# A retention layer with a gated feed-forward layer: two running sums moved ahead, two groups opened together, seven half-size products reordered

## The chip, the cores and the metric

The kernel runs on one core of a Trainium2 chip. The metric is the device time of one execution in microseconds (us). A core has engines that run side by side, each with a queue that it works off in order: TensorE (PE in the profile; its weight loads are PEld), VectorE (DVE), ScalarE (ACT), GpSimd (POOL) and SyncE (SP), which issues most transfers. They wait for each other through semaphores. TensorE writes into PSUM, which has eight banks; VectorE and ScalarE carry results out of it.

## The reference, cut to what matters

```python
scores = scale * np.matmul(q, k.transpose(0, 1, 3, 2))       # q, k, v: 8 x 8 x 576 x 64
Dmat = np.where(rel >= 0, gamma ** rel, 0.0)                 # rel = row - column, gamma per head
attn_out = np.matmul(scores * Dmat, v)
x = attn_out.transpose(0, 2, 1, 3).reshape(4608, 512)
out = (x @ w_a) * (x @ w_b) @ w_out                          # 512 -> 1536 -> 512
```

## The kernel before, in words

**Retention by groups.** The 4608 rows are cut into 18 groups of 256. Fourteen and two more are halves of a batch's first 512 rows; groups 15 and 17 (`LEFT`) collect the last 64 rows of four batches each. In a group, the rows of one 64-row part meet each other through masked scores, and meet all earlier rows through a state, a running sum of key times value products. So a group needs these sets of small TensorE products, each 64x64 on a quarter of the array:

- `keyed` (line 646): the key-value products `kv`, into two PSUM banks of the pool `ps_ffn`. VectorE then adds them up in four steps, `add(0)` to `add(3)` (line 690, tile `sums`). The two banks come free when the last two steps have read them. ScalarE turns sums into `states`.
- `matched` (line 725): the scores `sc`, which VectorE masks (line 743, tile `sT`).
- `open_outputs` (line 796): the products of queries and states open the output `o`; behind it ScalarE reads two columns (`fence`, line 803), for which the next set waits.
- `close_outputs` (line 806): the products of masked scores and values finish `o`; ScalarE copies it to `xT` (line 819) later, when the code pops a list `later`.

`stretch(into, outof)` (line 828) issues such sets in one go: it opens the outputs of group `outof`, forms `kv` and `sc` of group `into`, and closes `outof`. A group in `LEFT` has no `kv`, so its stretch has only `sc` and the closing; `outof` is opened by a separate call, `open_alone`, some products earlier. Group 17 is opened and closed by two more calls.

**Feed-forward by blocks.** Blocks of 512 rows (and two of 256) follow each other on TensorE. For each of twelve columns F there are four products `pa` (line 1365) and four `pb` (line 1383), each 128x512; ScalarE copies `pa` to `ha` (line 1376) and VectorE multiplies `ha` with `pb` to `hT` (line 1388). `pa`, `pb`, `kv` and others share the four banks of `ps_ffn`. From row 1536 on, the second layer goes by seven half-size products (`rows_mixed`, tile `m`), fed by sums of `hT` on VectorE (`row_sums`, line 957, bf16, both operands in SBUF), and its results are put together on GpSimd (line 1046) and VectorE (lines 1056 and 1063). In the last two blocks (rows 3584 and 4096) pairs of columns of the first layer go by seven half-size products as well (`layer_mixed`): ways 1 to 7, into banks `lm` (ways 1, 6, 7, 4), `ls` (5, 3) and `la` (2). ScalarE keeps a copy after ways 1 (`straight`), 6 (`crossed`) and 5 (`less`), line 1205, and the next way into that bank waits for it. They use sums of weights (`combos`, line 1151) and of rows (`rows`, line 1168), made on VectorE.

**What sets the order.** The order on each engine is that of the code. A list `todo` names a place, counted in 128x512 products, for each stretch; the stretches are put between two columns F. VectorE's smaller work stands in `jobs`, each with a class and a cost, and `work(budget)`, called behind each `hT`, issues jobs of the lowest class until the budget of 1.0 is used. The four `add` steps cost 0.5 each and have the lowest class, so behind a stretch two of them go after the next `hT` and two after the one that follows. `ORDER_MIDDLE` and `ORDER` (lines 1236 and 1288) are the hand-written orders of the half-size products of the last two blocks.

Of the kernel before, what the change touches and what calls it, by code (L numbers as in the profile page):

```python
# [10 lines left out]
FP32 = mybir.dt.float32  # L11
# [7 lines left out]
def kernel(  # L19
# [10 lines left out]
    nc = tc.nc  # L30
# [7 lines left out]
    HP = H // 2  # L38
# [6 lines left out]
    NP = NTOK // 256  # L45
    LEFT = {NP - 3: 0, NP - 1: 1}
# [57 lines left out]
    ps_ffn = pool("ps_ffn", 4, PS)  # L104
    opening, ps_sc, ps_o = ExitStack(), {}, {}
# [39 lines left out]
    def half(i):  # L145
        return slice(64 * i, 64 * i + 64)
# [120 lines left out]
    def pair_tables(step):  # L267
# [6 lines left out]
        else:  # L274
            for h in (2 * step - 2, 2 * step - 1):
# [8 lines left out]
                for n in range(FIRST)]  # L284
    second = sum_pool.tile([128, FIRST, HP, 64], FP32, tag="sums",
                           name="second")
# [20 lines left out]
    later = []  # L307
# [5 lines left out]
    jobs, copies_due = [], []  # L313
# [18 lines left out]
    def settle():  # L332

        while later:
            later.pop(0)()
        for job in [job for job in jobs if job[0] in (0, 2)]:
            jobs.remove(job)
            job[2]()
        pass_on(math.inf)

    def flush():
        while later:
            later.pop(0)()
        work(math.inf)
        pass_on(math.inf)
# [379 lines left out]
    def matched(n):  # L725
        qkT = of(transposed, n)
        sc = [ps_sc[0].tile([128, HP, 2, 64], FP32, tag="sc", name=f"sc{on}")
              for on in (0, 1)]
        begun = Begun()
        for c in range(HP):  # L730
            for kp in (0, 1):
                for a, r in QUADS:
                    on = r ^ a
                    nc.tensor.matmul(sc[on][half(a), c, kp, :],  # L734
                                     qkT[half(on), 1, kp, c, half(a)],
                                     qkT[half(on), 0, kp, c, half(a)],
                                     start=begun.first(on, a), stop=True,
                                     skip_group_check=True)
        sT = st_pool.tile([128, 2, HP, 2, 64], BF16, tag="sT", name="sT2")
        scored[FIRST + n, "pair"] = sT  # L740

        def masked(on):
            nc.vector.tensor_tensor(  # L743
                sT[:, on].rearrange("p c k s -> p (c k) s"),
                sc[on].rearrange("p c k s -> p (c k) s"),
                mask3.unsqueeze(1).to_broadcast([128, 2 * HP, 64]),
                op=ALU.mult)
        return masked

    def from_states(n, o, begun):  # L750
        qkT = of(transposed, n)
        st = states_of.pop(n)
        first = first_of.pop(n, st[:, 0])
        for c in range(HP):
            for kp in (0, 1):
                for a, r in QUADS:
                    i = 2 * kp + a
                    if block_of(n, i) == 0:
                        continue
                    on = r ^ a  # L760
                    own = st[:, i] if i else first
                    nc.tensor.matmul(o[a][half(r), c, kp, :],  # L762
                                     own[half(on), c, :],
                                     qkT[half(on), 0, kp, c, half(a)],
                                     start=begun.first(a, r), stop=True,
                                     skip_group_check=True)

    def keys_into(n, o, begun):
        vb = of(natural, n)[1]
        sT = of(scored, n)  # L770
        for c in range(HP):
            for kp in (0, 1):
                for a, r in QUADS:
                    v0 = kp * DM + c * 128 + 64 * r
                    nc.tensor.matmul(o[half(r), a, c, kp, :],  # L775
                                     vb[half(a), v0:v0 + 64],
                                     sT[half(a), r ^ a, c, kp, :],
                                     start=begun.first(a, r), stop=True,
                                     skip_group_check=True)

    def rows_at(n, kp):

        x = x_of(place(n) * 256, 256)
        if n < MIXED:
            return x.rearrange("p c (q a s) -> p q a c s",
                               q=2, a=2)[:, kp]
        return x.rearrange("p c (k q a s) -> p q a c k s",
                           k=2, q=2, a=2)[:, kp]
# [4 lines left out]

    opened = {}

    def open_outputs(n):

        o = ps_o[0].tile([128, 2, HP, 2, 64], FP32, tag="o", name="o2")
        begun = Begun()
        from_states(n, [o[:, a] for a in (0, 1)], begun)  # L800

        kp = int(0 in (block_of(n, 0), block_of(n, 1)))
        nc.scalar.copy(fence, o[:, :, 0, kp, 0])
        opened[n] = o, begun

    def close_outputs(n):

        o, begun = opened.pop(n)
        keys_into(n, o, begun)

        def kept(kp):
            x = rows_at(n, kp)
            at = o[:, :, :, kp]
            if n < MIXED:
                by = qs_1[:, :, 128 * kp:128 * kp + 128].rearrange(
                    "p c (a s) -> p a c s", a=2)
                nc.vector.tensor_tensor(x, at, by, op=ALU.mult)
                return
            nc.scalar.copy(x, at.rearrange("p a c (s k) -> p a c k s", k=2))  # L819

        later.append(lambda: kept(0))
        later.append(lambda: kept(1))

    def open_alone(n):
        (settle if n >= NP - 2 else flush)()
        open_outputs(n)

    def stretch(into, outof):

        (settle if into == NP - 1 else flush)()  # L830
        if into == FIRST:
            ps_next("pair", 2)
        if into in LEFT:
            masked = matched(into)
            close_outputs(outof)
            later.append(lambda: masked(0))
            later.append(lambda: masked(1))
            return
        if into == 5:
            convert, convert_swapped = keyed(into, False,  # L840
                                             lambda: open_outputs(outof))
            pop()
            pop()
        else:
            if outof is not None:
                open_outputs(outof)
            convert, convert_swapped = keyed(into, outof is None)
        masked = matched(into)
        if outof is not None:
            close_outputs(outof)  # L850
        if into == 4:
            later.append(later.pop(1))
            behind.extend([lambda: masked(0), convert, lambda: masked(1)])
            behind.extend(convert_swapped(apart=True))
            return
        if into > MIXED:
            jobs.extend((0, 0.5, add) for add in later[:4])
            jobs.append((0, 0, lambda: copies_due.extend(
                [convert, convert_swapped])))
            jobs.extend((0 if into % 2 else 2, 0.7,  # L860
                         lambda on=on: masked(on)) for on in (0, 1))
            copies_due.extend(later[4:])
            later.clear()
            return
        later.append(lambda: (convert(), masked(0)))
        later.append(lambda: (convert_swapped(), masked(1)))
# [21 lines left out]
    begun = {}  # L888
# [281 lines left out]
    def layer_mixed(tok0, xT, hT):  # L1170
# [63 lines left out]

    MIDDLE = (NTOK - 1024,)
    ORDER_MIDDLE = (
        (1, 0), (5, 0), (2, 0), (6, 0), (1, 1), (3, 0), (7, 0), (5, 1),
        (2, 1), (6, 1), (4, 0), ("a", 4), (3, 1), (7, 1), ("b", 4),
        ("a", 5), (4, 1), ("b", 5)) + tuple(
            (w, F) for F in range(6, 12) for w in "ab")  # L1240
    SHARE_MIDDLE = {1: 0, 5: 0, 2: 0, 6: 0.4, 3: 0, 7: 0.4, 4: 0, "b": 1}
# [1 line left out]
    def middle_layer(tok0, xT, hT, sums):  # L1243
# [3 lines left out]
        for way, at in ORDER_MIDDLE:  # L1247
# [33 lines left out]
            if done == 5:  # L1281
# [3 lines left out]
            work(SHARE_MIDDLE[way])  # L1285
            yield last, way in ("b", 4) and not underway

    ORDER = ((1, 0), (5, 0), (2, 0), (6, 0), (1, 1), (3, 0), (7, 0), (5, 1),
             (2, 1), (6, 1), (4, 0), ("a", 4), (3, 1), (7, 1), ("b", 4),
             ("a", 5), (4, 1), ("b", 5),  # L1290
             (1, 3), (5, 3), (2, 3), (6, 3), (1, 4), (3, 3), (7, 3), (5, 4),
             (2, 4), (6, 4), (4, 3), ("a", 10), (3, 4), (7, 4), ("b", 10),
# [135 lines left out]
    fence = const.tile([128, 2], FP32)  # L1428
# [95 lines left out]
    starts, at = {}, 0.0  # L1524
# [60 lines left out]
    for n in range(8, NP, 2):  # L1585
        todo += [(starts[n] - (92 if n == 16 else 116 if n > 8 else 112), stretch, (n + 1, n)),
                 (starts[n] - (52 if n > 8 else 48), stretch, (n + 2, n + 1))
                 if n + 2 < NP else
                 (starts[n] - 52, close_outputs, (n + 1,))]
    todo += [(starts[n - 1] - 124, open_alone, (n - 1,)) for n in LEFT]  # L1590
    todo += [(starts[NP - 2] - 60, open_alone, (NP - 1,))]
    placed = {args[0]: at for at, fn, args in todo if fn is stretch}
    casts = {3: 116, 4: 116.15, 5: 141, 6: 200, 7: 253, 8: 283, 9: 376,
             10: 412}
# [12 lines left out]
             (411.95, store_held, (2,)), (412.3, load_pair, (11, (K, V))),  # L1607
             (458, load_pair, (12,)), (447, store_held, (2,)),
             (456, store_held, (2,))]
    LATE = 8, 8, 8, 50, 8  # L1610
    CAST_A, TURN_A, CAST_B, TURN_B = 96, 58, 96, 58
    for n in range(11, NP):
# [51 lines left out]
```

## Time and profile before

| what | value |
|---|---|
| time, median of 3 | 318.93 us (318.79 to 319.56) |
| time of the profiled execution | 318.84 us |
| span of its instructions | 317.1 us, 1.74 us less than its time |
| TensorE clock granted | 1.00 |
| blocks from row 1536, 2048, 2560, 3072, 3584, 4096 begin at about | 121, 154, 188, 220, 253, 284 us |
| `hT` products on VectorE (line 1388) | 96, mean 618 ns |
| `sums` (line 690) | 44, mean 423 ns |
| values by decay on GpSimd (line 615) | 17, mean 1729 ns |

The page counts busy time by engine and gives, for each group of instructions, the idle time before it and what ended it. The timeline lists an engine's instructions in order of time with their starts, and behind some of them in brackets how long the engine had been idle and for what; `issue` means that the profile shows no wait. The TensorE rows there merge instructions of one kind that follow each other (x4), so the distance of two starts tells how long the first kind held the array.

### The profile page before, as it was taken

To read this page: it belongs to the slowest core of one execution; us is meant where nothing else is said; L and a number is where in the kernel's file an instruction comes from. 1 tells how busy PE (TensorE), PEld (TensorE's weight loads), DVE (VectorE), ACT (ScalarE), POOL (GpSimd) and SP (SyncE) were. 2 spreads that over 40 slices of the span, in tenths; PEclk is the share of its full clock that TensorE was granted. 3 is DMA by queue.
4 is the path that set the end of the run, shared out by engine and by line. 5 is a ranking of instruction groups with operands and counts; after the bars stand their busy time and mean duration, and the time that the engine had idled before them with its cause. 6 is when DMAs were issued, how large, how long until landed. Compare 5 with 4: busy or idle time off the path is not lost.

```text
span 317.1 us, 9394 instructions
## 1 busy us (share of the span) xinstructions
PE 310.5 (98%) x3871; PEld 190.9 (60%) x3871; DVE 217.9 (69%) x426; ACT 150.5 (47%) x333; POOL 169.3 (53%) x187
## 2 busy tenths in 40 slices
PE   8999999999999999999999999999999999999995
PEld 3554457768544554548644775468446874587774
DVE  5845346767858572479668867787677886758873
ACT  6745346536435364454455535535434554335630
POOL 3990068654995678473796079605980350035313
PEclk9999999999999999999999999999999999999999
DMA  8999999999999999999999996983530030004004
GB/s 215 255 203 207 253 237 181 189 211 172 212 176 225 225 227 200 234 212 268 192 262 220 175 234 133 194 181 105 148 68 3 2 132 2 2 0 134 1 3 132
DMA packets 144795, 50.94 MB, mean 161 GB/s; under 512 B 126576, under 2 KB 141680, under 8 KB 144752
## 3 DMA queue, kind: packets, MB, share of 16 engines
q1 hardware_dynamic: 138272, 45.10, 71.2%
q0 software_dynamic: 5808, 4.72, 9.5%
q8 instruction: 30, 0.49, 0.7%
q10 hardware_dynamic: 672, 0.52, 0.5%
q14 instruction: 13, 0.11, 0.1%
HBM read 37.75 MB, written 9.44 MB: 149 GB/s over the span
## 4 chain that ended last, share of the span: by engine, by line
PE 90%; DVE 3%; DMA 2%; POOL 1%; SPq 1%; ACT 1%; issue 1%; DVEq 0%; ACTq 0%; POOLq 0%
PE pb L1383 23%; PE pa L1365 22%; PE m L1023 16%; PE po L1409 8%; PE lm L1198 3%; PE pa L1253 2%; PE pb L1253 2%; DMA vf<-in_v_dram 2%; PE o L762 2%; PE sc L734 2%; PE po L909 2%; PE ls L1198 1%; PE o L775 1%; PE kv L663 1%; SPq L182 1%; PE pb L1307 1%
## 5 line engine op out<-in xcount | busy, mean ns | idle before, releaser
L1388 DVE TENSOR_TENSOR hT<-ha,pb 128x512 bf16<-128x512 bf16 (+1 forms) x96 | 59.3, 618 | 55.6 <-PE pb L1383 46.8
L1383 PE MATMUL pb<-xT,wb_sb 128*128 128x512 bf16 (+1 forms) x384 | 87.0, 352 | 0.1
L1365 PE MATMUL pa<-xT,wa_sb 128*128 128x512 bf16 (+1 forms) x376 | 85.2, 352 | 0.0
L1376 ACT CAST ha<-pa 128x512 bf16<-128x512 f32 (+1 forms) x96 | 50.9, 531 | 68.3 <-PE pa L1365 65.7
L1383 PEld LDWEIGHTS <-wb_sb 128*128 128x128 bf16 x384 | 37.4, 98 | 36.2 <-issue 1.9
L1365 PEld LDWEIGHTS <-wa_sb 128*128 128x128 bf16 x376 | 35.7, 98 | 32.4 <-DVE sums L690 0.2
L1046 POOL TENSOR_TENSOR osb<-crossed,straight 128x512 f32<-128x512 f32 x12 | 15.2, 1269 | 73.5 <-ACT crossed L1035 73.3
L615 POOL TENSOR_TENSOR vb<-vf,vs 128x1024 bf16<-128x1024 f32 (+1 forms) x17 | 29.4, 1729 | 4.9 <-DMA vf<-in_v_dram 3.3
L578 POOL TENSOR_TENSOR qkb<-qf,qs 64x1024 bf16<-64x1024 f32 x12 | 23.3, 1942 | 15.8 <-DMA qf<-in_q_dram 11.1
L1023 PEld LDWEIGHTS <-hT 128*128 128x128 bf16 x288 | 28.1, 98 | 4.4
L1409 PE MATMUL po<-wo_sb,hT 128*128 128x512 bf16 x120 | 27.8, 379 | 0.0
L1023 PE MATMUL m<-wo_sums,hsum 128*128 128x256 bf16 x216 | 25.7, 273 | 0.0
L583 POOL TENSOR_TENSOR qkb<-qf,qs 64x512 bf16<-64x512 f32 x24 | 24.8, 1055 | 0.7
L957 DVE TENSOR_TENSOR hsum<-hT 128x512 bf16<-128x512 bf16 (+2 forms) x51 | 23.5, 489 | 0.3
L1023 PEld LDWEIGHTS <-hsum 128*128 128x128 bf16 x216 | 21.1, 98 | 2.5
L743 DVE TENSOR_TENSOR sT<-sc,mask 128x512 bf16<-128x512 f32 x30 | 19.8, 682 | 0.0
L690 DVE TENSOR_TENSOR sums<-kv,sums 128x256 f32<-128x256 f32 x44 | 18.6, 423 | 1.4
L608 POOL CAST qkb<-kf 64x512 bf16<-64x512 f32 (+1 forms) x34 | 19.1, 588 | 0.9
L604 POOL CAST qkb<-kf 64x1024 bf16<-64x1024 f32 (+1 forms) x17 | 16.2, 950 | 5.5 <-DMA kf<-in_k_dram 4.6
L819 ACT CAST xT<-o 128x512 bf16<-128x512 f32 x24 | 13.9, 588 | 10.3 <-PE o L775 10.3
L1409 PEld LDWEIGHTS <-hT 128*128 128x128 bf16 x120 | 11.2, 98 | 12.4
L1023 PE MATMUL m<-wo_sums,hT 128*128 128x256 bf16 x144 | 16.9, 273 | 0.0
(155 smaller groups left out, 434.7 us busy)
## 6 DMA issues: line engine op xcount, KB each, us to landing
qf<-in_q_dram SPq DMA_DIRECT2D x32, 256.0 KB, 4.5
vf<-in_v_dram SPq DMA_DIRECT2D x32, 256.0 KB, 5.2
kf<-in_k_dram SPq DMA_DIRECT2D x31, 256.0 KB, 4.8
out_dram<-osb SPq DMA_DIRECT2D x9, 512.0 KB, 3.4
out_dram<-osb SPq DMA_DIRECT2D x22, 128.0 KB, 2.9
wo_sb<-in_moe_w_out_dram POOLq DMA_DIRECT2D x3, 512.0 KB, 15.7
out_dram<-osb SPq DMA_DIRECT2D x6, 256.0 KB, 4.3
qf<-in_q_dram SPq DMA_DIRECT2D x8, 128.0 KB, 4.1
```

The costliest lines, as they stand in the source:

```text
L578: nc.gpsimd.tensor_tensor(per_head(qkb[0:64, Q]), per_head(t[0:64]), by[0:64].unsqueeze(2).to_broadcast([64, 2 * H, D]), op=ALU.mult)
L583: nc.gpsimd.tensor_tensor(per_head(qkb[64:128, Q])[:, 1 - r::2], per_head(t[64:128])[:, r::2], by[64:128, r::2].unsqueeze(2).to_broadcast( ...
L608: nc.gpsimd.tensor_copy(to[:, :, 1 - r], fro[:, :, r])
L615: nc.gpsimd.tensor_tensor(vb[:, e].rearrange("p (h d) -> p h d", d=D), t[:, e].rearrange("p (h d) -> p h d", d=D), decay[:, at], op=ALU.mult)
L743: nc.vector.tensor_tensor(sT[:, on].rearrange("p c k s -> p (c k) s"), sc[on].rearrange("p c k s -> p (c k) s"), mask3.unsqueeze(1).to_bro ...
L957: lambda e=ways[i]: nc.vector.tensor_tensor(*e[:3], op=e[3]))
L1023: nc.tensor.matmul(to, rows, cols, start=(begins and p == 0), stop=True, skip_group_check=True)
L1365: nc.tensor.matmul(pa[:, 0:n], wa_sb[:, c, fs], xT[:, c], start=(c == 0), stop=(c == NC - 1))
L1376: nc.scalar.copy(ha[:, 0:n], pa[:, 0:n])
L1383: nc.tensor.matmul(pb[:, 0:n], wb_sb[:, c, fs], xT[:, c], start=(c == 0), stop=(c == NC - 1))
L1388: nc.vector.tensor_tensor(hT[:, F, 0:n], has[F][:, 0:n], pb[:, 0:n], op=ALU.mult)
L1409: nc.tensor.matmul(po, hT[:, F, u * 128:(u + 1) * 128], wo_sb[:, F], start=(F == 0), stop=(F == NF - 1))
```

## The change

1. `NOW = 2`: in the stretches into groups after 6, the first two `add` steps are issued at the end of the stretch itself, ahead of the next `hT`, and the other two stay jobs.
2. In the stretches into groups 15 and 17 the outputs of both groups are opened: `outof` in two banks of `ps_ffn` (tiles `os0`, `os1`, with a `fence` and two copies each in place of one), `into` in the bank pair of `o`. Then come `sc` of `into` and the closing of `outof`. The calls of `open_alone` for groups 14, 16 and 17 go; group 17 is closed eight products earlier (`close_alone`).
3. In the first six pair-steps of `ORDER_MIDDLE` and of the first half of `ORDER`, way 2 of the first pair and ways 1 and 6 of the second come ahead of ways 5 and 3 of the first.

```diff
+    def open_outputs(n, apart=False):
+
+        if apart:
+            o = [ps_ffn.tile([128, HP, 2, 64], FP32, tag="ab", name=f"os{a}")
+                 for a in (0, 1)]
+        else:
+            o = ps_o[0].tile([128, 2, HP, 2, 64], FP32, tag="o", name="o2")
...
+        if apart:
+            for a in (0, 1):
+                nc.scalar.copy(fence[:, a:a + 1], o[a][:, 0, kp, 0:1])
+        else:
+            nc.scalar.copy(fence, o[:, :, 0, kp, 0])
...
+            if apart:
+                for a in (0, 1):
+                    nc.scalar.copy(x[:, a], o[a][:, :, kp].rearrange(
+                        "p c (s k) -> p c k s", k=2))
+                return
...
+    def close_alone(n):
+        settle()
+        close_outputs(n)
...
         if into in LEFT:
+            open_outputs(outof, True)
+            open_outputs(into)
             masked = matched(into)
             close_outputs(outof)
...
-            if outof is not None:
+            if outof is not None and outof not in opened:
                 open_outputs(outof)
...
         if into > MIXED:
-            jobs.extend((0, 0.5, add) for add in later[:4])
+            for add in later[:NOW]:
+                add()
+            jobs.extend((0, 0.5, add) for add in later[NOW:4])
...
-        (1, 0), (5, 0), (2, 0), (6, 0), (1, 1), (3, 0), (7, 0), (5, 1),
-        (2, 1), (6, 1), (4, 0), ("a", 4), (3, 1), (7, 1), ("b", 4),
+        (1, 0), (2, 0), (1, 1), (6, 0), (5, 0), (6, 1), (7, 0), (3, 0),
+        (5, 1), (2, 1), (4, 0), ("a", 4), (3, 1), (7, 1), ("b", 4),
         ("a", 5), (4, 1), ("b", 5)) + tuple(
...
-                 (starts[n] - 52, close_outputs, (n + 1,))]
-    todo += [(starts[n - 1] - 124, open_alone, (n - 1,)) for n in LEFT]
-    todo += [(starts[NP - 2] - 60, open_alone, (NP - 1,))]
+                 (starts[n] - 60, close_alone, (n + 1,))]
...
+    NOW = 2
```

More of the change, by code (lines that the diff above doesn't have):

```diff
@@ L774, in keys_into @@
                     v0 = kp * DM + c * 128 + 64 * r
-                    nc.tensor.matmul(o[half(r), a, c, kp, :],
+                    nc.tensor.matmul(o[a][half(r), c, kp, :],
                                      vb[half(a), v0:v0 + 64],
@@ L794 @@
     opened = {}
-    def open_outputs(n):
-        o = ps_o[0].tile([128, 2, HP, 2, 64], FP32, tag="o", name="o2")
+    def open_outputs(n, apart=False):
[4 more added lines that the diff above has]
+            o = ps_o[0].tile([128, 2, HP, 2, 64], FP32, tag="o", name="o2")
         begun = Begun()
-        from_states(n, [o[:, a] for a in (0, 1)], begun)
+        from_states(n, o if apart else [o[:, a] for a in (0, 1)], begun)
         kp = int(0 in (block_of(n, 0), block_of(n, 1)))
-        nc.scalar.copy(fence, o[:, :, 0, kp, 0])
+        if apart:
[3 more added lines that the diff above has]
+            nc.scalar.copy(fence, o[:, :, 0, kp, 0])
         opened[n] = o, begun
@@ L808, in close_outputs @@
         o, begun = opened.pop(n)
-        keys_into(n, o, begun)
+        apart = isinstance(o, list)
+        keys_into(n, o if apart else [o[:, a] for a in (0, 1)], begun)
         def kept(kp):
             x = rows_at(n, kp)
+            if apart:
[3 more added lines that the diff above has]
+                return
             at = o[:, :, :, kp]
@@ L824, in open_alone @@
     def open_alone(n):
-        (settle if n >= NP - 2 else flush)()
+        flush()
         open_outputs(n)
+    def close_alone(n):
+        settle()
+        close_outputs(n)
     def stretch(into, outof):
@@ L1286, in middle_layer @@
             yield last, way in ("b", 4) and not underway
-    ORDER = ((1, 0), (5, 0), (2, 0), (6, 0), (1, 1), (3, 0), (7, 0), (5, 1),
-             (2, 1), (6, 1), (4, 0), ("a", 4), (3, 1), (7, 1), ("b", 4),
+    ORDER = ((1, 0), (2, 0), (1, 1), (6, 0), (5, 0), (6, 1), (7, 0), (3, 0),
+             (5, 1), (2, 1), (4, 0), ("a", 4), (3, 1), (7, 1), ("b", 4),
              ("a", 5), (4, 1), ("b", 5),
```

## The prediction

> **What bounds the kernel now.** I read the page first: the busy line, then the engine shares of the chain that ended last.
>
> ```profile
> PE 310.5 (98%) x3871; PEld 190.9 (60%) x3871; DVE 217.9 (69%) x426; ACT 150.5 (47%) x333; POOL 169.3 (53%) x187
> PE 90%; DVE 3%; DMA 2%; POOL 1%; SPq 1%; ACT 1%; issue 1%; DVEq 0%; ACTq 0%; POOLq 0%
> ```
>
> TensorE is the bound, and the change leaves it all its products. So it can only shorten TensorE's gaps: dearer spells where small products break a chain of large ones, and waits for the engines that free PSUM banks. I went through TensorE's timeline from 106 us on for starts later than the rows before them allow, then looked at what VectorE, ScalarE and GpSimd did there. In undisturbed stretches four 128x512 products take 0.865 us.
>
> The first view is TensorE's timeline at the stretch into group 15 (block 3072), then at a lone opening in the next block.
>
> ```profile
> 239.71 1.03 PE L1383 MATMUL pb<-xT,wb_sb 128*128 128x512 bf16 x4
> 240.66 0.45 PE L762 MATMUL o<-qkT,left_states 64*64 64x64 bf16 x32
> 240.94 0.44 PE L663 MATMUL kv<-vb,qkb 64*64 64x64 bf16 x32
> 241.19 0.47 PE L734 MATMUL sc<-qkT 64*64 64x64 bf16 x32
> 241.48 0.45 PE L775 MATMUL o<-sT,vb 64*64 64x64 bf16 x32
> 241.86 1.04 PE L1365 MATMUL pa<-xT,wa_sb 128*128 128x512 bf16 x4
> ...
> 269.91 1.03 PE L1253 MATMUL pb<-xT,wb_sb 128*128 128x512 bf16 x4
> 270.87 0.45 PE L762 MATMUL o<-qkT,left_states 64*64 64x64 bf16 x32
> 271.25 1.04 PE L1253 MATMUL pa<-xT,wa_sb 128*128 128x512 bf16 x4
> ```
>
> From `pb` to the next `pa` pass 2.15 us with 128 small products between and 1.34 with 32; less 0.865 that is 1.285 and 0.475. So a small product costs 0.81/96, or 0.0084, and each insertion about 0.20 on top. An insertion of 64 measures 0.74, which fits.
>
> The second view is VectorE, TensorE and GpSimd around the `kv` stretch of block 2560.
>
> ```profile
> 193.38 1.90 POOL L615 TENSOR_TENSOR vb<-vf,vs 128x1024 bf16<-128x1024 f32 x1
> 193.47 2.09 DVE L1151 TENSOR_TENSOR combos<-wb_sb 128x512 bf16<-128x512 bf16 x1
> ...
> 195.66 1.03 PE L1365 MATMUL pa<-xT,wa_sb 128*128 128x512 bf16 x4
> 195.93 0.69 DVE L1388 TENSOR_TENSOR hT<-ha,pb 128x512 bf16<-128x512 bf16 x1 [0.36 <-PE pb L1383]
> 196.54 0.88 DVE L690 TENSOR_TENSOR sums<-kv,sums 128x256 f32<-128x256 f32 x2
> 196.68 0.53 PEld L1383 LDWEIGHTS <-wb_sb 128*128 128x128 bf16 x3 [0.27 <-issue]
> ...
> 197.81 0.69 DVE L1388 TENSOR_TENSOR hT<-ha,pb 128x512 bf16<-128x512 bf16 x1 [0.39 <-PE pb L1383]
> 198.55 0.53 PEld L1383 LDWEIGHTS <-wb_sb 128*128 128x128 bf16 x3 [0.27 <-issue]
> ```
>
> The `pa` at 195.66 allows `pb` at 196.52; it starts at 196.67, when `hT` has been read out (0.15 late). The next `pb` is 0.15 late again. While `kv` holds two of the four banks, each `pb` waits for the `hT` just before it. `combos`, 0.52 at 191.75, took 2.09 and ended 0.28 behind GpSimd's L615 at 195.57. It cost nothing, since VectorE then still idled 0.36 for `pb`.
>
> The third view is the opening of the last block but one.
>
> ```profile
> 252.77 0.38 PE L1198 MATMUL lm<-xT,wa_sb 128*128 128x256 bf16 x2
> ...
> 254.57 0.59 ACT L1205 COPY less<-ls 128x512 f32<-128x512 f32 x1 [0.52 <-DVE osb L1063]
> ...
> 255.21 0.60 PE L1198 MATMUL ls<-xT,combos 128*128 128x256 bf16 x4
> ...
> 257.44 0.38 PE L1198 MATMUL lm<-rows,wa_sb 128*128 128x256 bf16 x2
> ```
>
> Way 3 starts 0.24 late at 255.21, waiting for the copy `less` that started at 254.57; in the last block the same place is 0.30 late (286.85).
>
> **Joint openings.** Block 3072 has insertions of 24, 64 and 128, and will have 120 and 96: the same 216 products, one insertion less. Block 3584 has 32, 64, 32 and 32, and will have 128 and 32: the same 160, two less. Taken insertion by insertion the sums are 2.485 and 2.26 (-0.23), 2.15 and 1.755 (-0.395): **-0.62** together. Against this stand the fences. Now the closing starts 0.82 after the opening (240.66 to 241.48) and the `kv` set covers ScalarE's fence (0.51 after the opening, 0.16 long). In the joint stretch three fences go through ScalarE, with two sets of 32 for cover, one of them the opening behind which the last fence stands. Small ScalarE copies follow each other after 0.10. I take **+0.13** for both stretches; bounds 0 (all covered) and +0.25. The copies to `xT` become four of 128x256 instead of two of 128x512, about 0.2 more of ScalarE per group; it idles there (0.67 ahead of the copy at 242.00), so nothing, and up to the same 0.2 if ScalarE is late at the next `pa`. `os0` and `os1` take two `ffn` banks, so later bank waits change: by the rows, the next but one `pa` needs an `ha` that ends 0.03 before. Nothing. SP's order is the same in both kernels and the transposes for groups 15 and 17 are issued tens of us earlier (201.18 for 15), so the earlier `sc` waits for no DMA.
>
> **Order of half-size products.** Ten sets of four, 0.435 each, precede way 4 of the first pair: at least 4.35. Before it starts at 4.67 (252.77 to 257.44) and 4.72. In the new order way 3 is eighth, not sixth, so `less` has two sets (0.87) more, but ways 6 and 1 are closer to each other, and ScalarE's copies of 0.59, 0.48 apart, follow without a pause; the copies ahead of way 7 and of the second way 6 leave about 0.1 of wait. I get 4.47 to 4.50: **-0.42** for both blocks; bounds 0 and -0.54 (both waits gone and nothing new).
>
> **Sums ahead.** With two `add` right behind the stretch, the other two follow the next `hT`, not the one after, so `kv` frees its banks one column earlier. The first late `pb` of each block stays (its bank still needs that `hT`), the second goes: three blocks with a `kv` stretch in this form (stalls at 134.24, 165.41 and 198.55), 0.15 each: **-0.46**. What is queued behind is the trouble. In block 2560 VectorE is held until 195.57; then come two sums (0.88), where `hT` stood: `hT` starts at about 196.35, ends at 197.02, and `pb` starts at 197.04 instead of 196.67: **+0.36** (bounds 0 and +0.5). In block 2048, VectorE has fewer jobs at the front, so the two `combos` at 176.99 to 177.86 move up behind the `hT` of column 6, at about 169.4, under GpSimd's L608 and L615, which there end at 170.06 and 172.04. If they are held as at 193.47, `hT` of column 7 ends near 172.3 where its bank is needed at 172.03: **+0.3** (bounds 0, since in block 2560 such a hold cost nothing, and +0.8, a whole `combos` and `hT` more). I take 0.3, as the same pair of engines is in the same state. Block 2560's own moved `combos` fall under no long GpSimd row: nothing.
>
> The Trainium skill speaks against this part: its page "SBUF — State Buffer", section "SBUF: two separate sides", makes the port that VectorE and GpSimd share an exclusive lock, held for a whole instruction, and the 2.09 at 193.47 agrees. Were the port shared in turns instead, both holds would shrink and the time would be about 317.5.
>
> **Sum.** -0.62 + 0.13 - 0.42 - 0.46 + 0.36 + 0.30 = **-0.71**. The profiled execution took 318.84 (span 317.1 and 1.74 around it), 0.09 under the median of the runs, so 318.13: I forecast **318.1**.
>
> **Rivals.** A: only one of the two holds on VectorE costs its 0.3 to 0.36: 317.8. For it: block 2048's is by a GpSimd start that itself depends on VectorE's sums. B: neither does: 317.47. Against it: the row at 193.47. C: the sums free nothing, because the second `pb` still waits for its `hT` (the ring turns so that its bank is not one of `kv`'s): +0.46, **318.6**; against it, all four banks go round in order. D, slower: ScalarE reaches the fences late. A copy of 0.59 ahead of them, and a fence of 0.16, delay the closing in both joint stretches, for every fence is on TensorE's path: 2 x 0.75 is +1.5 on 318.1, **319.6**. It decides once ScalarE is more than 0.3 late per stretch (then the switches' gain is gone). For it: `ha` is copied 0.75 before the first small product there. Against it: ScalarE idled 0.68 ahead of the fence at 241.17.
>
> **How the numbers follow.** Forecast, both holds: 0.42. A 0.26, B 0.16, C 0.09, D 0.07. Lowest with B and the far ends of the first two parts: 317.2; highest, short of D's full price, C with uncovered fences and a full hold, 319.1. About 0.3%, 0.96 us, is what a measurement of this kernel can tell from no change: below 317.97 is faster, above 319.89 slower. Faster: B, nearly all of A, and a few of the forecast's low cases: 0.40. Slower: part of D: 0.04. The rest, 0.56, within.
>
> **What would show it.** In the profile after: from the last large product before the joint stretch to the first one behind it, 128 products with 1.29 and 120 with 1.22 beyond 0.865, plus 0.07 for fences; way 4 at +4.5 in both last blocks; one late `pb` per `kv` stretch instead of two; in block 2560 `pb` about 0.5 late behind held `combos` and two sums; in block 2048 a late `pb` near 172. It would be wrong if a fence starts over 0.3 late, or if `combos` held under GpSimd appear in other columns.

## The result, and the profile after

The changed kernel takes 318.32 us (median of 22 runs, 317.78 to 319.79); the kernel before, in 22 runs of the same kind, 319.38 (318.63 to 320.06). The ratio is 0.9971 (95% interval 0.9961 to 0.9981): faster by 0.93 us, with 0.61 to 1.24 in the interval, or 0.3%. The forecast was 318.1, in a range of 317.2 to 319.1. The profiled execution of the changed kernel spans 316.8 us, 0.3 less than that of before.

The page of the changed kernel, engine shares of the chain that ended last:

```profile
PE 88%; DVE 3%; issue 2%; DMA 2%; SPq 2%; ACT 2%; DVEq 0%
```

TensorE is still the bound. So the question is again which of its gaps went and which came. The lines of the code have moved: `combos` is now line 1173, `hT` 1410, `pa` 1387, `pb` 1405, the half-size products 1220.

Timeline of the kernel after, TensorE and ScalarE at the joint stretch of block 3584, then TensorE at what is left for group 17 (start, length, engine, line):

```profile
262.05 1.03 PE L1275 MATMUL pb<-xT,wb_sb 128*128 128x512 bf16 x4
262.30 0.38 ACT L1251 CAST ha<-lm 128x256 bf16<-128x256 f32 x1
263.01 0.45 PE L762 MATMUL os<-qkT,states 64*64 64x64 bf16 x32
263.28 0.46 PE L762 MATMUL o<-qkT,left_states 64*64 64x64 bf16 x32
263.51 0.22 ACT L809 COPY fence<-os 128x1 f32<-128x1 f32 x2 [0.83 <-PE os L762]
263.57 0.47 PE L734 MATMUL sc<-qkT 64*64 64x64 bf16 x32
263.86 0.47 PE L775 MATMUL os<-sT,vb 64*64 64x64 bf16 x32
263.89 0.16 ACT L811 COPY fence<-o 128x2 f32<-128x2 f32 x1 [0.16 <-PE o L762]
264.26 1.04 PE L1275 MATMUL pa<-xT,wa_sb 128*128 128x512 bf16 x3
...
271.27 0.45 PE L775 MATMUL o<-sT,vb 64*64 64x64 bf16 x32
271.65 1.04 PE L1275 MATMUL pa<-xT,wa_sb 128*128 128x512 bf16 x3
```

From `pb` to `pa` pass 2.21 us, 1.345 beyond 0.865; 128 small products cost 1.285 in the kernel before, so the stretch is 0.06 dearer. No row shows a wait for a fence: the first two end at 263.73, the closing starts at 263.86, 0.29 behind `sc` as in the kernel before (241.19 to 241.48), and the third fence starts behind it, at 263.89. That the 0.06 is the price of the fences is therefore not shown. ScalarE had idled 0.83 ahead of the first fence. The two lone insertions of before are gone.

The opening of that block (the first way 1, the two copies that were in question, way 3, way 4):

```profile
253.23 0.38 PE L1220 MATMUL lm<-xT,wa_sb 128*128 128x256 bf16 x2
...
255.75 0.60 ACT L1227 COPY less<-ls 128x512 f32<-128x512 f32 x1
256.23 0.62 ACT L1227 COPY crossed<-lm 128x512 f32<-128x512 f32 x1
256.41 0.60 PE L1220 MATMUL ls<-xT,combos 128*128 128x256 bf16 x4
...
257.72 0.38 PE L1220 MATMUL lm<-rows,wa_sb 128*128 128x256 bf16 x2
```

Way 4 starts at +4.49 (4.67 before). `less` ends at 256.35 and way 3 starts 0.06 later; by the weight loads of TensorE way 3 is still about 0.055 late, where it was 0.24 late before, and way 7 ahead of it by as much, behind the copy `crossed` that started at 255.28.

VectorE, GpSimd and the weight loads of `pb` (PEld) in block 2048, at the place where nothing was late before, and in block 2560:

```profile
169.30 2.73 DVE L1173 TENSOR_TENSOR combos<-wa_sb,combos 128x512 bf16<-128x512 bf16 x2
169.79 1.95 POOL L615 TENSOR_TENSOR vb<-vf,vs 128x1024 bf16<-128x1024 f32 x1
...
171.95 0.67 DVE L1410 TENSOR_TENSOR hT<-ha,pb 128x512 bf16<-128x512 bf16 x1
...
172.68 0.53 PEld L1405 LDWEIGHTS <-wb_sb 128*128 128x128 bf16 x3 [0.60 <-issue]
...
193.60 1.90 POOL L615 TENSOR_TENSOR vb<-vf,vs 128x1024 bf16<-128x1024 f32 x1
193.69 2.09 DVE L1173 TENSOR_TENSOR combos<-wb_sb 128x512 bf16<-128x512 bf16 x1
...
195.71 0.94 DVE L690 TENSOR_TENSOR sums<-kv,sums 128x256 f32<-128x256 f32 x2
196.56 0.68 DVE L1410 TENSOR_TENSOR hT<-ha,pb 128x512 bf16<-128x512 bf16 x1
...
197.30 0.53 PEld L1405 LDWEIGHTS <-wb_sb 128*128 128x128 bf16 x3 [0.67 <-issue]
```

Both times `combos` ends 0.28 to 0.29 behind the end of L615 (171.74 to 172.03, 195.50 to 195.78). The `hT` behind it (and in block 2560 behind two sums) is late, and `pb` with it: 0.48 and 0.55.

**The steps, one by one.** All kernels here have the same number of large weight loads (1767), so the n-th of one trace can be set beside the n-th of another, and the time between two loads is called a step here. Up to load 600, at about 118 us, the work of all kernels here is the same, and their traces differ by up to 1.2 us there. Behind it steps of like code come back within 0.06, except small stalls of 0 to 0.3 among the products of three stretches (block 1536's first, 2048's and 2560's second) and one of 0.25 to 0.3 near 150 us in two of twelve traces (that of `e6` is left out here). "Again" are the repeats `e8` and `e11` below.

| step (us) | before | before, again | after | after, again |
|---|---|---|---|---|
| to the second `pb` behind a first stretch, 3 blocks, each | 1.87 | 1.87 | 1.72 | 1.72 |
| two products and the wait between them, near 172 | 0.43 | 0.43 | 0.91 | 0.85 |
| the same, near 197 | 0.58 | 0.58 | 0.98 | 0.99 |
| block 3072, openings and first stretch | 18.49 | 18.49 | 18.60 | 18.60 |
| block 3072, second stretch | 4.77 | 4.77 | 4.53 | 4.53 |
| block 3584, opening | 2.47 | 2.47 | 2.29 | 2.29 |
| block 3584, stretches | 18.84 | 18.84 | 18.49 | 18.49 |
| last block, opening | 2.54 | 2.54 | 2.31 | 2.31 |
| from load 600 to the last | 195.02 | 195.34 | 194.53 | 194.40 |

Added up: sums -0.45 + 0.45 + 0.40 = +0.40; joint openings -0.13 - 0.35 = -0.48; order -0.18 - 0.23 = -0.41; together **-0.49** by steps that recur, and -0.71 by the mean of two traces each, which holds some of the stalls that come and go.

### The profile page after: what moved, and what is told of

Same layout as the page of the kernel before. It is cut to its first block, busy times and chain, and to the rows that moved or that the text cites. A ratio compares the mean times of both kernels' runs of the same rounds, so it can differ in the third digit from the quotient of the medians.

```text
span 316.8 us, 9373 instructions
## 1 busy us (share of the span) xinstructions
PE 306.2 (97%) x3836; PEld 191.1 (60%) x3871; DVE 218.7 (69%) x426; ACT 151.0 (48%) x339; POOL 169.6 (54%) x187
## 4 chain that ended last, share of the span: by engine, by line
PE 88%; DVE 3%; issue 2%; DMA 2%; SPq 2%; ACT 2%; DVEq 0%
PE pb L1405 21%; PE pa L1387 20%; PE m L1045 17%; PE po L1431 7%; PE lm L1220 3%; PE pa L1275 2%; PE pb L1275 2%; DMA qf<-in_q_dram 2%; SPq L182 2%; PE ls L1220 2%; PE po L931 2%; PE sc L734 1%; PE o L762 1%; PE o L775 1%; PE kv L663 1%
## 5 line engine op out<-in xcount | busy, mean ns | idle before, releaser
L1387 PE MATMUL pa<-xT,wa_sb 128*128 128x512 bf16 (+1 forms) x358 | 82.8, 351 | 1.8 <-issue 1.1
L615 POOL TENSOR_TENSOR vb<-vf,vs 128x1024 bf16<-128x1024 f32 (+1 forms) x17 | 29.4, 1731 | 4.1 <-DMA vf<-in_v_dram 1.9
L1431 PE MATMUL po<-wo_sb,hT 128*128 128x512 bf16 x113 | 26.7, 379 | 0.8 <-issue 0.6
L979 DVE TENSOR_TENSOR hsum<-hT 128x512 bf16<-128x512 bf16 (+2 forms) x51 | 22.1, 462 | 0.4
L1078 DVE TENSOR_TENSOR less<-m,crossed 128x512 f32<-128x512 f32 (+1 forms) x14 | 8.3, 613 | 13.2 <-ACT crossed L1057 13.2
```

The lines of the kernel that those rows point to most:

```text
L615: nc.gpsimd.tensor_tensor(vb[:, e].rearrange("p (h d) -> p h d", d=D), t[:, e].rearrange("p (h d) -> p h d", d=D), decay[:, at], op=ALU.mult)
L979: lambda e=ways[i]: nc.vector.tensor_tensor(*e[:3], op=e[3]))
L1387: nc.tensor.matmul(pa[:, 0:n], wa_sb[:, c, fs], xT[:, c], start=(c == 0), stop=(c == NC - 1))
L1431: nc.tensor.matmul(po, hT[:, F, u * 128:(u + 1) * 128], wo_sb[:, F], start=(F == 0), stop=(F == NF - 1))
```

## The experiments

Each was timed in 5 rounds beside the kernel before on the same chip, and profiled. The theory, from the traces: the joint openings and the order bring what the switches and waits cost; the sums lose, because VectorE is held under GpSimd. The rival: the timed gain of 0.93 is larger than that of the traces, so the sums bring a gain in ordinary runs.

**One part alone.** `e1_sums_alone`, the kernel before with

```diff
-            jobs.extend((0, 0.5, add) for add in later[:4])
+            for add in later[:2]:
+                add()
+            jobs.extend((0, 0.5, add) for add in later[2:4])
```

> Part 1 alone. Theory: in the profile three late second pb go (0.15 each, -0.45), and two held combos on VectorE bring waits of about 0.48 near 172 us and 0.40 more near 197 us; net +0.4 us, ratio to before about 1.001. Rival: the holds cost only the profiled run anything and the sums bring what they were meant to bring: -0.45 us, ratio 0.9986.

Measured: ratio 1.0027 (1.0007 to 1.0047). The second `pb` are at 1.72 in all three blocks, the steps near 172 and 197 took 0.85 and 0.99. Slower alone: the rival falls.

`e2_joint_alone`, part 2 of the change on the kernel before (sums and orders as before):

> Part 2 alone. Theory: block 3072 shorter by 0.12 to 0.16, block 3584 by 0.33, a switch of 0.20 less in the first and two in the second, minus 0.05 to 0.08 for the fences of each joint stretch: -0.47 us, ratio 0.9985. Rival (fences late): no gain, ratio 1.000 or above, and the closing products of the joint stretches start more than 0.3 late.

Measured: 0.9985 (0.9976 to 0.9994). The steps of block 3072 take 18.60 and 4.48 (+0.11 and -0.29), block 3584's 18.49 (-0.35): -0.53. Late fences as a rival fall.

`e3_order_alone`:

```diff
-        (1, 0), (5, 0), (2, 0), (6, 0), (1, 1), (3, 0), (7, 0), (5, 1),
-        (2, 1), (6, 1), (4, 0), ("a", 4), (3, 1), (7, 1), ("b", 4),
+        (1, 0), (2, 0), (1, 1), (6, 0), (5, 0), (6, 1), (7, 0), (3, 0),
+        (5, 1), (2, 1), (4, 0), ("a", 4), (3, 1), (7, 1), ("b", 4),
```

(and the same in `ORDER`)

> Part 3 alone. Theory: way 4 of the first pair starts about 0.2 sooner in each of the last two blocks, -0.41 us, ratio 0.9987. Rival (the wait only moves to another way): below 0.1 us, ratio 1.000.

Measured: 0.9995 (0.9984 to 1.0007). The time alone can't tell the two apart; the trace can: the openings take 2.28 and 2.31, -0.19 and -0.23, and nothing gives it back.

`e4_no_sums`, the change with `NOW = 0`:

> The change without part 1. Theory: -0.47 and -0.41 stand without the +0.4 of the sums: -0.88 us, ratio 0.9972 to before, 0.4 us faster than the whole change would be by its profile. Rival (the sums bring a gain in ordinary runs): slower than the whole change, ratio 0.9985.

Measured: 0.9969 (0.9957 to 0.9981), 317.86 us. The steps of parts 2 and 3 are all there, those near 172 and 197 are 0.43 and 0.58 again. Its steps give -0.94, its time -0.99.

**Is it GpSimd that holds VectorE?** Two edits that take one of the two away. `e5_combos_moved`, other places for `combos` in blocks 2048 and 2560:

```diff
-                     + i % 4 * LATE[4], combine,
+                     + PLACES[i // 4][i % 4], combine,
...
+    PLACES = ((0, 8, 48, 48), (0, 0, 48, 48), (0, 8, 16, 24), (0, 8, 16, 24))
```

> The whole change, and the sums of weights that were held are issued elsewhere: in block 2560 the second behind the first, in blocks 2048 and 2560 the third and fourth behind the row sums. Theory: the late pb of 0.48 near 172 us goes, the one of 0.55 near 197 falls to 0.15; -0.88 us against the change in the profile, so -1.3 us against before, ratio 0.9958. Rival (VectorE has too much work there, whichever operations they are): a late pb of some 0.4 stays in the same columns, ratio as the change's, 0.998.

Measured: 0.999 (0.9968 to 1.0011), short of the gain expected. Both late `pb` are gone as expected (0.43 and 0.58, the latter with the 0.15 of before), but a wait that was in neither kernel comes in. Timeline of VectorE and TensorE in this kernel, end of block 2048:

```profile
177.73 0.88 DVE L1173 TENSOR_TENSOR combos<-wa_sb,combos 128x512 bf16<-128x512 bf16 x2
...
178.53 0.41 DVE L687 COPY sums<-kv 128x256 f32<-128x256 f32 x1
179.41 0.42 DVE L690 TENSOR_TENSOR sums<-kv,sums 128x256 f32<-128x256 f32 x1 [0.47 <-PE pb L1405]
179.75 0.68 DVE L1410 TENSOR_TENSOR hT<-ha,pb 128x512 bf16<-128x512 bf16 x1
...
180.48 1.69 PE L1045 MATMUL m<-wo_sums,hT 128*128 128x256 bf16 x14 [0.40 <-DVE hT L1410]
```

The moved `combos` and the two early sums of the second stretch stand ahead of the last `hT`, and the second layer waits 0.56 for it. What the second sum waited for in its 0.47 can't be told from these rows: the products it reads had long ended.

`e6_values_first`, VectorE's order as in the change; on GpSimd the values come first:

```diff
+        if n > 10:
+            values()
         if n >= MIXED:
             decayed_queries(paired[n].pop(Q))
```

(`values` holds the lines that stood behind the keys; up to group 10 it is called there)

> The whole change with VectorE's order untouched; only GpSimd's differs: from group 11 on it forms the values by decay (line 615, 1.9 us) ahead of queries and keys, so that shorter operations lie under the sums of weights. Theory (a sum of weights that starts under a GpSimd operation ends 0.28 behind that operation's end): the second sum of block 2560 ends near 194.4 instead of 195.8, the third and fourth of block 2048 near 171.1 instead of 172.0, both late pb fall to 0.15 and 0 to 0.1; -0.8 to -0.88 us against the change, ratio 0.9959 to before. Rival (they are long for a reason of their own, their operands or their place): 2.1 and 2.7 us stay, and so do both waits.

Measured: 1.0122 (1.0082 to 1.0163), far slower, and yet its steps near 172 and 197 are 0.43 and 0.58: with shorter GpSimd operations over them, the same `combos` took less, in block 2048 1.59 for two (kernel of this run, whose times are 4 us later):

```profile
173.87 1.59 DVE L1179 TENSOR_TENSOR combos<-wa_sb,combos 128x512 bf16<-128x512 bf16 x2
174.01 1.17 POOL L618 CAST qkb<-kf 64x1024 bf16<-64x1024 f32 x1
```

These end 0.28 behind the end of L618 (175.18 to 175.46): the hold followed GpSimd's operation, with VectorE's order as it was. So it is GpSimd. What made this run slow is in the main the same thing in another place (VectorE, GpSimd and TensorE at the end of block 1536):

```profile
144.24 1.90 POOL L596 TENSOR_TENSOR vb<-vf,vs 128x1024 bf16<-128x1024 f32 x1 [10.32 <-PE o L768]
144.39 2.30 DVE L985 TENSOR_TENSOR hT<-hT 128x1024 bf16<-128x1024 bf16 x1
...
146.10 2.35 POOL L578 TENSOR_TENSOR qkb<-qf,qs 64x1024 bf16<-64x1024 f32 x1
146.62 4.50 DVE L985 TENSOR_TENSOR hsum<-hT 128x512 bf16<-128x512 bf16 x3
...
148.51 2.32 POOL L583 TENSOR_TENSOR qkb<-qf,qs 64x512 bf16<-64x512 f32 x2
...
152.35 1.89 PE L1051 MATMUL m<-wo_sb,hT 128*128 128x256 bf16 x8 [2.51 <-DVE hT L985]
```

GpSimd idles 10.3 us until products of TensorE let go of what the values wait for, and queries and keys, queued behind, now run beside VectorE's `hsum`: three of them take 4.50 us, one after the other held, and the second layer waits; this step takes 6.84 us in place of 2.40. About 1 us of that is not the wait itself: behind the 2.51 us in which TensorE stood, its granted clock was 0.50 from 153 to 155 us (1.00 up to 152), and the weight loads came 0.21 apart instead of 0.11. The hold came back where it had not been before.

**Which stretches need early sums?** `e7_all_sums_now`, `e5_combos_moved` with `NOW = 4`:

> As the run with the moved sums of weights, and all four sums of states right behind the stretch instead of two. Theory: they take 1.76 us in which VectorE waits for pb anyway; both kv banks are then free before the second pa and pb after the stretch, so the remaining late pb of three blocks (0.15 each) goes too: -0.45 us more, -1.8 us against before, ratio 0.9944. Rival: hT stands behind four sums and pb waits for it: nothing gained or up to 0.3 us per block lost, ratio 0.996 to 0.999.

Measured: 1.0059 (1.0041 to 1.0076). The first half of it came true: all six late `pb` of the first stretches are gone. But in the second stretch of a block the sums are ahead of the last `hT`; VectorE and TensorE in this kernel:

```profile
178.13 1.34 DVE L690 TENSOR_TENSOR sums<-kv,sums 128x256 f32<-128x256 f32 x3 [0.47 <-PE pb L1405]
179.07 2.14 PE L1045 MATMUL m<-wo_sums,hT 128*128 128x256 bf16 x18 [1.36 <-DVE sums L690]
```

The steps into the three second layers get 1.54, 1.17 and 0.52 longer than before.

`e8_change_again` is the changed kernel once more:

> The changed kernel once more beside the others. Theory: in the profile the steps between 120 us and the end come back within 0.05 each (late pb of 0.48 and 0.55; blocks 3072 and 3584 shorter by 0.12 and 0.35; way 4 sooner by 0.18 and 0.23), net -0.5 us, ratio 0.9985; what differs between profiles lies ahead of 120 us. Rival (the profiled run was an odd one, the change gains 0.9): one of the two late pb is missing in the repeat, ratio 0.997.

Measured: 0.9976 (0.9953 to 0.9998); the table above has its steps. All recur; the rival falls.

`e9_first_stretch_four`, `e5_combos_moved` with early sums in the first stretches only:

```diff
-            for add in later[:NOW]:
+            now = NOW if into % 2 else 0
+            for add in later[:now]:
                 add()
-            jobs.extend((0, 0.5, add) for add in later[NOW:4])
+            jobs.extend((0, 0.5, add) for add in later[now:4])
...
+    NOW = 4
```

> As the run with the moved sums of weights, but the sums of states go ahead only in the first kv stretch of a block, all four of them; in the second stretch they wait as in the kernel before. Theory (the sums in a second stretch save no bank wait and stand ahead of the last hT, for which the second layer waits): the waits of 0.56 at 180.5 and of 1.5, 1.2 and 0.75 where the second layers begin go, all late pb of the three first stretches are gone; -0.9 for the sums, -0.47, -0.41: -1.8 us against before, ratio 0.9944. Rival (the moved sums of weights alone hold up the block's end): a wait of some 0.5 stays near 180 us, ratio 0.996.

Measured: **0.9948** (0.9933 to 0.9964), 316.98 us: faster than both kernels, by the traces too (192.91 from load 600 to the last, against 195.02 before and 194.53 after the change). The wait near 180 is gone (that step takes 3.69, as before), so the moved `combos` alone do no harm. Timeline, block 2560, where after the change 0.55 was lost:

```profile
192.71 1.85 DVE L690 TENSOR_TENSOR sums<-kv,sums 128x256 f32<-128x256 f32 x4
192.74 1.90 POOL L615 TENSOR_TENSOR vb<-vf,vs 128x1024 bf16<-128x1024 f32 x1
...
195.67 1.03 PE L1406 MATMUL pb<-xT,wb_sb 128*128 128x512 bf16 x4
195.69 0.68 DVE L743 TENSOR_TENSOR sT<-sc,mask 128x512 bf16<-128x512 f32 x1
```

The four sums lie in the time in which VectorE would wait for `pb`, under the same L615, and are not held: 0.46 each. They have one operand in PSUM, `combos` has both in SBUF. L615 itself took 1.90, as beside the held `combos`.

`e10_first_stretch_two`, the same with `NOW = 2`:

> The same with two sums ahead in the first stretch instead of four. Theory: one late pb of 0.15 stays in each of three blocks; -0.45, -0.47, -0.41: -1.33 us against before, ratio 0.9958, and no wait of 0.56 at 180.5. Rival as for the run with four: that wait stays, ratio 0.9975.

Measured: 0.9954 (0.9942 to 0.9966), 317.47 us; one late `pb` of 0.15 per block is back, as expected.

`e11_before_again`:

> The kernel before, once more. Theory: ratio 1.000; its profile has the six late pb of 0.15 and the two of 0.24 and 0.30 again, and differs from the first one only ahead of 120 us and by under 0.2 in the small products of the second stretches. Rival (waits move from run to run): other late pb appear.

Measured: 1.0006 (0.9995 to 1.0018). The late `pb` and openings are the same to 0.01; a stall of 0.25 near 150 us, in the second layer, is new; it was in one other trace of twelve. Its cause was not looked for.

## Why the prediction was right

**Sum and range.** The three parts and their signs came as forecast, but the size of the whole was met in part by luck. Forecast -0.71; the recurring steps give -0.49, the two traces of each kernel -0.71, the times -0.93 (-0.61 to -1.24) and in the repeat -0.76 (-0.06 to -1.50). So the steps fall short of the forecast, the sums being too cheap in it, and the times lie beyond it. In absolute terms 318.32 is 0.2 from 318.1, yet the kernel before had 319.38 beside it, 0.45 above the 318.93 from which the forecast started. The prediction took 0.3% as the least that can be told from no change; 22 runs of each kernel gave an interval 0.2% wide. Where the 0.1 to 0.4 between recurring steps and times come from stays open. The runs of single parts scatter by as much around their steps (`e1` +0.86 for +0.4, `e3` -0.16 for -0.42).

**Joint openings, -0.62 + 0.13 = -0.49 forecast; -0.53 alone, -0.48 in the change.** Insertion by insertion: 128 products cost 1.345 where 1.285 was taken from the row, so 0.06 more, where 0.065 per stretch was set down for fences. The stretch of 120 in block 3072 costs 1.33, 0.11 above the 1.22 taken. The sum of both, 0.17, is near the +0.13, but that fences are what it pays for is not shown: in both joint stretches the closing starts 0.29 behind `sc` (226.75 to 227.04 in block 3072), after the first two fences have ended and ahead of the third, which the prediction counted. The 2.26 for 120 and 96 products is 0.04 above what the prediction's own 0.20 and 0.0084 give. The stretch of 96 is 0.05 longer with early sums than without.

**Order, -0.42; measured -0.41.** Way 4 comes at +4.49 (4.47 to 4.50 forecast). The 0.1 of wait that is left has the size forecast and one of its two places: it lies ahead of way 7, as forecast, and of way 3, not of the second way 6.

**Sums, +0.20; measured +0.40.** The second late `pb` goes in all three blocks (-0.45), the first stays. Block 2560's wait was worked out as 0.52 and came as 0.55. The mis-sized term is block 2048: +0.30 forecast, 0.42 to 0.48 measured. There the mechanism was right (two `combos` moved up behind the `hT` of column 6 and ended 0.29 behind L615), but the sum was not: from the L615 that the prediction names, ending at 172.04, and a hold as at 193.47, `combos` end at 172.32 and `hT`, 0.67 long, at 172.99, not near 172.3. By its own rows the price was about 0.96, above its bound of +0.8. It came out at half of that because in the changed kernel L615 ended sooner, at 171.74, so that `hT` ended at 172.62, and because TensorE needed the bank later, at 172.19. That +0.30 was no further off is luck. The third pair of moved `combos`, in block 2560, was put under no long GpSimd row; it did fall under L615:

```profile
202.04 1.90 POOL L615 TENSOR_TENSOR vb<-vf,vs 128x1024 bf16<-128x1024 f32 x1
...
202.48 2.20 DVE L1173 TENSOR_TENSOR combos<-wb_sb,combos 128x512 bf16<-128x512 bf16 x2
```

This is what the prediction's last line named as a sign of being wrong, held `combos` in another column. It cost TensorE nothing, by chance: `hT` was in time for its bank.

**What was not seen.** That the sums in second stretches save no wait and take VectorE's slack ahead of the second layer. In the change this cost nothing; once `combos` were also there it cost 0.56. The rival in which the sums free nothing falls with the second `pb` at 1.72, that of late fences with ScalarE's 0.83 of idle time ahead of them. The rival with only one hold (317.8) and that with none (317.47) are answered by the rows: both holds recur. The one with shared turns falls too: `combos` ends 0.28 behind L615, and in block 2560 L615 takes its 1.90 whether `combos` or the sums run beside it. The Trainium skill's exclusive lock (page "SBUF — State Buffer", section "SBUF: two separate sides") agrees with that, and with the sums that pass: beside modes that use two ports, that section names VectorE operations with two inputs in SBUF.

## What to carry to other kernels

A job that is moved ahead on VectorE brings others forward behind it: work out which GpSimd operation lies over each of them, and which `hT` stands behind. Move early only where the bank is waited for (here the first stretch of each block, not the second), and put what GpSimd can hold where nobody waits behind it. Where small products break a chain of large ones, count insertions as well as products: here each cost about 0.2 us on top of 0.0084 per product.

## What the runs showed of the hardware that I had not expected

Three `hsum` of 128x512, each held in turn under GpSimd, took 4.50 us (1.08 for three at 181.14 in the run with the moved `combos`): holds add up, and TensorE, after it had stood for 2.51 us, had a granted clock of 0.50 for some 3 us. A sum with one operand in PSUM took 0.46 under the same kind of GpSimd operation (L615) that stretched `combos` from 0.52 to 2.09. And the first 60 us, the same work in all kernels here, differ by up to 1.0 us between traces, the last 200 us of one kernel by 0.1 to 0.3, so a step of 0.2 us is read from the trace, not from the time.
